# First loads, warm-up products and slab statistics at the head of a two-branch kernel

## The chip, the cores and the metric

One core of one Trainium2 chip. The metric is the device time of one execution in microseconds (us). The span that a profile shows is about 1.75 us shorter than the time of the same execution (201.1 and 202.87 us for the kernel before).

## The reference, cut to what matters

```python
def reference(A_x, A_w_r, A_w_i, B_x, B_w_gate, B_w_up, B_w_down):   # x: 1 x 2048 x 640
    x  = A_x
    xn = _layernorm(x, axis=-1)
    s  = irfft2(rfft2(xn) * (w_r + 1j * w_i))                          # spectral branch
    g  = _silu((_gelu(xn @ w_gate) * (xn @ w_up)) @ w_down)            # 640 -> 1536 -> 640
    return x + s * g
```

The kernel cuts the 2048 rows into 16 slabs of 128. The spectral branch is done by matrix products: a "fold" of each slab pair, then products with tables (T, FM, FT and others). A *gate* or *up* product is one with w_gate or w_up, a *down* product one with w_down.

## The kernel before: the parts that the argument touches

Names in the profiles: uT is the product of the gate and up branches that the down products read, ge the gelu of the gate, mb the input of a fold, BU the folds' results read back from HBM. A bank (tags sp, pg, pu) is a piece of the memory that TensorE writes to. The tail is all that follows the last product. A transfer is issued by an engine's queue and has landed when all its data are there.

A small scheduler in the kernel takes every operation with modelled durations, its inputs and buffers, and writes out one fixed order for each engine. `rank` orders what is ready at the same time.

The head. Slab 0 is loaded by ScalarE's queue, everything else by SyncE's (`dma` calls `nc.sync.dma_start`). `keep_warm` emits dummy products. `land` is the scheduler's guess of a landing time in ns.

```python
    nc.scalar.dma_start(out=X[:, 0, :], in_=xv[:, 0, :])
    ...
    load_w(Wg, gv, g_in, 0, 2, land=4690)
    load_x(1, 2, land=5200)
    load_w(Wu, uv, u_in, 0, 2, land=6790)
    load_x(2, 3, land=7280)
    load_x(3, 4, land=7750)
    t = add(blank, "DVE", (330, 400), (0, -9), new=[idle])
    t = warmed = keep_warm(6, [t])
```

The first four slabs go to TensorE untouched by the normalisation (tile XR). Their gate and up products are corrected later, when each row's mean and scale have come back from HBM, broadcast to all partitions, as the tile RB (512 KB):

```python
    rb_in = dma(RB..., D5....partition_broadcast(P), (0, -5, 1), 524288, after=[rs])
```

Of the kernel before, what the change touches and what calls it, by code (L numbers as in the profile page):

```python
# [12 lines left out]
BF16 = mybir.dt.bfloat16  # L13
ACT = mybir.ActivationFunctionType
ALU = mybir.AluOpType
P = 128
# [98 lines left out]
class Plan:  # L115
# [12 lines left out]
    def add(self, emit, eng, cost, rank, after=(), new=(), use=(), size=0, slow=1.0, hold=0, order=(), lag=0, land=0):  # L128
        engs = eng if isinstance(eng, dict) else {eng: cost}
        t = Task(emit=emit, engs=engs, rank=rank, after=list(after), new=list(new), size=size, slow=slow, hold=hold, order=list(order), lag=lag, land=land,  # L130
                 seq=len(self.tasks))
        for s in (*new, *use):
            s.users.append(t)
        self.tasks.append(t)
        return t
# [72 lines left out]
def c_pe(*ns):  # L208
    occ = sum(n / 2.4 + 2.5 for n in ns)
    return occ, occ + 240  # L210


def c_act(n, psum=True, extra=0):
    return 0.833 * n + 60 + extra, 0.833 * n + 200 + extra


def c_dve(n, rate=2, psum=False, extra=0):
    d = ((120 if psum else 58) + n / rate) / 0.96 + extra
    return d + 10, d + 130
# [3 lines left out]
def kernel(  # L223
# [11 lines left out]
    nc = tc.nc  # L235
# [32 lines left out]
    Wg = persist.tile([P, 5, F], BF16)  # L268
    Wu = persist.tile([P, 5, F], BF16)
# [7 lines left out]
    def flat(t):  # L277
        names = "abcde"[:len(t.shape) - 1]
        if len(names) == 1:
# [4 lines left out]
                uT=16, ge=3, th=2, G2=12, W=3, xb=1)  # L284
    plan = Plan(BUFS, dict(PE=700, DVE=900, ACT=3500, POOL=900, SP=750))
    add = plan.add

    def place(slot, shape, dt=BF16):
        if slot.tag in ("sp", "pg", "pu"):
            slot.tile = psum.tile([P, *shape], dt, tag=slot.tag, name=slot.tag)  # L290
        else:
            slot.tile = work.tile([P, *shape], dt, tag=slot.tag, name=slot.tag, bufs=BUFS[slot.tag])
        return slot.tile

    def copy_on(e, out, in_):
        return nc.scalar.copy(out=out, in_=in_) if e == "ACT" else nc.vector.tensor_copy(out=out, in_=in_)  # L296
# [5 lines left out]
    def dma(out, in_, rank, size, after=(), new=(), use=(), slow=1.0, land=0):  # L302
        return add(lambda e: nc.sync.dma_start(out=out() if callable(out) else out, in_=in_() if callable(in_) else in_),  # L303
                   "SP", (430, 430), rank, after=after, new=new, use=use, size=size, slow=slow, land=land)

    gv = B_w_gate.rearrange("(c p) f -> p c f", p=P)
    uv = B_w_up.rearrange("(c p) f -> p c f", p=P)
# [4 lines left out]
    x_in, g_in, u_in, tab_in, d_in = {}, {}, {}, {}, {}  # L312
# [3 lines left out]
    def load_x(a, b, land=0):  # L316
        seq[0] += 1
        t = dma(X[:, a:b, :], xv[:, a:b, :], (0, -4, seq[0]), (b - a) * 163840, use=[sX], land=land)
        for n in range(a, b):
            x_in[n] = t  # L320
# [9 lines left out]
    def load_w(sb, view, got, a, b, land=0):  # L330
        cs = slice(a * P, b * P)
        seq[0] += 1
        w = dma(sb[:, :, cs], view[:, :, cs], (0, -4, seq[0]), (b - a) * 163840, slow=1.1, land=land)
        for t in range(a, b):
            got[t] = w

    def load_gu(a, b):
        load_w(Wg, gv, g_in, a, b)
        load_w(Wu, uv, u_in, a, b)
# [15 lines left out]
    nc.scalar.activation(out=warm, in_=warm, func=ACT.Gelu_apprx_tanh)  # L355
    for w in WF:
        nc.gpsimd.memset(w[:, :, :, L:LP], 0.0)
    idle, heat = Slot("uT"), Slot("sp")

    def blank(e):  # L360
        nc.vector.memset(place(idle, (512,)), 0.0)

    def keep_warm(n, after, rank=(0, -9), ns=425):
        def go(e):
            if heat.tile is None:
                place(heat, (2, 512))
            for k in range(n):
                nc.tensor.matmul(heat.tile[:, k % 2, :], lhsT=idle.tile[:, 0:P], rhs=idle.tile,
                                 start=True, stop=True, skip_group_check=True)
        return add(go, "PE", (n * ns, n * ns), rank, after=after, new=[] if heat.users else [heat], use=[idle] + ([heat] if heat.users else []))  # L370
    seq[0] += 1
    x_in[0] = add(lambda e: None, "SP", (1, 1), (0, -5), size=1, land=3620)
    load_w(Wg, gv, g_in, 0, 2, land=4690)
    load_x(1, 2, land=5200)
    load_w(Wu, uv, u_in, 0, 2, land=6790)
    load_x(2, 3, land=7280)
    load_x(3, 4, land=7750)
    t = add(blank, "DVE", (330, 400), (0, -9), new=[idle])
    t = warmed = keep_warm(6, [t])
    load_gu(2, 4)  # L380
    load_x(4, 6)
    load_tab("f1")
# [71 lines left out]
    def turn_raw(n1):  # L454
        pt = Slot("sp")

        def half():
            return pt.tile[:, 0, :].bitcast(BF16)[:, 0:D]

        def mm(e):  # L460
            place(pt, (2, 512))
            for c in range(5):
                nc.tensor.transpose(out=half()[:, c * P:c * P + P], in_=X[:, n1, c * P:c * P + P], identity=ident)
        a = add(mm, "PE", c_pe(*[140] * 5), (0, n1), after=[x_in[n1], warmed], new=[pt], use=[sX])
        if n1 == 0:
            keep_warm(2, [a], (0, 0, 0))
        raw[n1] = add(lambda e: copy_on(e, XR[:, :, n1 * P + (n1 > 0):(n1 + 1) * P + (n1 > 0)], half().rearrange("p (c n) -> p c n", c=5)),
                      {"ACT": c_act(640)} if n1 < 2 else {"ACT": c_act(640), "DVE": (415, 560)}, None, (0, n1), after=[a], use=[pt], hold={1: 1000}.get(n1, 200))
    for n1 in range(4):
        turn_raw(n1)  # L470

# [68 lines left out]
            outs.append(add(cp, either(640), None, (1, 2 * j + s), after=[a] + outs, new=[] if s else [A], use=[pa, A] if s else [pa]))  # L540
        stored[j] = dma(lambda: D2[:, 2 * j:2 * j + 2, :], lambda: A.tile, (0, -1, j), 327680, after=outs, use=[A], slow=1.1)

    lead = ("DVE", "ACT", "DVE", "ACT")
    for n1 in range(NSLAB):
        if n1 % 2 == 0:
            xn_of[n1 // 2] = Slot("s1")
# [18 lines left out]
    t = add(rows_pe, "PE", (215, 460), (0, 7), after=[*minused, turned[2]] + [roots[n1] for n1 in range(4)], new=[sr])  # L565
    t = add(lambda e: nc.vector.tensor_copy(out=place(rt, (P,), FP32)[0:8, :], in_=sr.tile[0:8, 0, 0:P]), "DVE", c_dve(128, 1, True), (0, 3.5), after=[t], new=[rt], use=[sr])
# [303 lines left out]
    uT, u_done, xr_in, step = {}, {}, {}, [0]  # L870
# [182 lines left out]
```

## Time and profile before

| | before |
|---|---|
| time, median of 3 | 202.65 us (202.62 to 202.78) |
| span of the profiled run | 201.1 us |
| TensorE busy | 195.2 us, 97% |
| its waits ahead of the tail | 1.2 (start), 0.4 (slab 1), 0.4 us (at 37 us) |

How to read it: TensorE is the bound, so a change can win only where TensorE stands still or runs slowly. The lines themselves stand in the prediction. One view that the prediction did not look at became the important one: the order in which SyncE issues transfers. Here is that part of its timeline in the kernel before, from 43 to 56 us (start, us, queue, line, kind, output<-input, count; the first number is when the issue starts, not when the data land):

```profile
43.45 0.53 SPq L303 DMA_DIRECT2D D<-mc  x1
...
44.77 0.48 SPq L303 DMA_DIRECT2D D<-mc  x1
...
47.38 0.57 SPq L303 DMA_DIRECT2D T<-tab_t  x1
...
50.68 0.53 SPq L303 DMA_DIRECT2D D<-mc  x1
51.27 0.44 SPq L303 DMA_DIRECT2D FM<-tab_fm  x1
51.75 0.73 SPq L303 DMA_DIRECT2D FT<-tab_ft  x1
```

`D<-mc` is a fold store, 320 KB each. Every table stands *behind* the store that is ready at that moment.

### The profile page before, as it was taken

What the parts mean: (1) busy time and instruction counts of PE and PEld (TensorE: products, weight loads), DVE (VectorE), ACT (ScalarE), POOL (GpSimd) and SP (SyncE); (2) the same over time, 40 slices, a digit from 0 to 9 for tenths busy, and PEclk for the clock granted to TensorE, in tenths of its full rate; (3) what the DMA queues carried; (4) which work ended last, traced back from release to release, by engine and by line L of the source; (5) the groups of instructions that cost most, each with busy time, mean ns of one, the idle gap of its engine ahead of it and who ended that gap; (6) DMA issues with size and microseconds to landing.
All of it is one profiled execution on the core that took longest, in us unless ns stands there. A gap on an engine that the chain in (4) does not pass through costs nothing.

```text
span 201.1 us, 4125 instructions
## 1 busy us (share of the span) xinstructions
PE 195.2 (97%) x1527; PEld 117.4 (58%) x1527; DVE 149.7 (74%) x320; ACT 127.2 (63%) x224; POOL 33.1 (16%) x73
## 2 busy tenths in 40 slices
PE   7999999999999999999999999999999999999992
PEld 2994444566544555677755555467765555457781
DVE  3789969999323249999998999933257788887774
ACT  3898997974632768778775766333466565766421
POOL 2412347596000000000000000000004122211210
PEclk9999999999999999999999999999999999999999
DMA  6999999569949677333244210117704332332432
GB/s 175 329 316 325 344 392 235 126 165 196 301 128 375 223 202 178 103 93 115 61 126 126 75 50 16 68 49 221 317 3 135 96 132 100 98 107 92 130 103 65
DMA packets 35894, 32.62 MB, mean 162 GB/s; under 512 B 10910, under 2 KB 32930, under 8 KB 35874
## 3 DMA queue, kind: packets, MB, share of 16 engines
q1 hardware_dynamic: 34434, 29.49, 49.1%
q0 software_dynamic: 1152, 2.66, 4.8%
q10 hardware_dynamic: 288, 0.20, 0.5%
q8 instruction: 12, 0.20, 0.4%
q14 instruction: 8, 0.07, 0.1%
HBM read 22.51 MB, written 9.19 MB: 158 GB/s over the span
## 4 chain that ended last, share of the span: by engine, by line
PE 79%; DMA 10%; SPq 4%; DVE 3%; issue 1%; ACT 1%; DVEq 0%
PE pg L886 19%; PE pu L886 19%; PE pg L970 13%; PE pu L970 12%; DMA X<-in_A_x_dram 6%; SPq L303 4%; DMA RB<-D 4%; PE sp L697 3%; PE sp L830 3%; PE sp L772 2%; PE sp L806 2%; PE sp L670 2%; PE sp L532 1%; PE sp L690 1%; PE sp L824 1%
## 5 line engine op out<-in xcount | busy, mean ns | idle before, releaser
L886 PE MATMUL pu<-xnT,Wu 128*128 128x512 bf16 (+1 forms) x245 | 57.6, 366 | 0.0
L886 PE MATMUL pg<-xnT,Wg 128*128 128x512 bf16 (+1 forms) x245 | 57.5, 366 | 0.0
L907 DVE TENSOR_TENSOR uT<-pu,ge 128x512 bf16<-128x512 f32 x46 | 31.7, 689 | 20.9 <-PE pu L886 18.4
L970 PEld LDWEIGHTS <-uT 128*128 128x128 bf16 x396 | 37.8, 98 | 14.1 <-issue 0.6
L903 ACT ACTIVATE ge<-pg 128x512 bf16<-128x512 f32 x46 | 27.4, 597 | 25.5 <-PE pg L886 25.0
L886 PEld LDWEIGHTS <-Wg 128*128 128x128 bf16 x285 | 25.2, 98 | 22.1
L886 PEld LDWEIGHTS <-Wu 128*128 128x128 bf16 x285 | 25.1, 98 | 21.8
L970 PE MATMUL pg<-Wd,uT 128*128 128x320 bf16 (+2 forms) x204 | 30.5, 293 | 0.4 <-ACT ge L903 0.4
L970 PE MATMUL pu<-Wd,uT 128*128 128x320 bf16 (+1 forms) x192 | 29.7, 297 | 0.0
L296 ACT CAST ma<-sp 128x644 bf16<-128x644 f32 (+1 forms) x32 | 23.4, 792 | 9.7 <-PE sp L830 7.9
L932 POOL COPY xr<-s 1x1 bf16<-1x1 bf16 x1 | 0.2, 182 | 101.8 <-DVE s L856 101.8
L933 POOL DMA_DIRECT2D xr<-in_A_x_dram x16 | 8.8, 552 | 32.3 <-DVE res L957 31.7
L296 ACT CAST IU<-sp 128x640 bf16<-128x640 f32 x16 | 10.9, 691 | 4.2 <-PE sp L772 4.1
L979 ACT ACTIVATE th<-pg 128x320 f32<-128x320 f32 (+2 forms) x17 | 7.3, 427 | 9.9 <-PE pg L970 8.9
L296 ACT CAST Vt<-sp 128x640 bf16<-128x640 f32 x16 | 10.8, 691 | 3.7 <-PE sp L806 3.7
L984 DVE SCALAR_TENSOR_TENSOR G<-th,pg 128x320 bf16<-128x320 f32 (+1 forms) x16 | 7.7, 479 | 7.1 <-ACT th L979 6.9
L979 ACT ACTIVATE th<-pu 128x320 f32<-128x320 f32 (+1 forms) x16 | 7.0, 438 | 9.2 <-PE pu L970 9.0
L984 DVE SCALAR_TENSOR_TENSOR G<-th,pu 128x320 bf16<-128x320 f32 (+1 forms) x16 | 7.7, 480 | 5.6 <-ACT th L979 5.3
L296 ACT CAST mc<-sp 128x640 bf16<-128x640 f32 x15 | 9.8, 694 | 2.3 <-PE sp L533 1.3
L433 POOL TENSOR_TENSOR RSTD<-MVA,mh 128x1 f32<-128x1 f32 x12 | 8.4, 697 | 4.5 <-DVE MVA L415 3.7
L848 DVE TENSOR_TENSOR mb<-ma 128x640 bf16<-128x640 bf16 x8 | 3.9, 493 | 6.9 <-ACT ma L296 6.9
L750 DVE TENSOR_TENSOR R<-Y 64x644 bf16<-64x644 bf16 x16 | 7.8, 490 | 0.4
(107 smaller groups left out, 252.9 us busy)
## 6 DMA issues: line engine op xcount, KB each, us to landing
BU<-D SPq DMA_DIRECT2D x8, 640.0 KB
D<-mc SPq DMA_DIRECT2D x8, 320.0 KB
D<-IU SPq DMA_DIRECT2D x8, 320.0 KB
xr<-in_A_x_dram POOLq DMA_DIRECT2D x16, 160.0 KB, 2.6
out_dram<-res SPq DMA_DIRECT2D x15, 160.0 KB
Wg<-in_B_w_gate_dram SPq DMA_DIRECT2D x6, 320.0 KB
Wu<-in_B_w_up_dram SPq DMA_DIRECT2D x6, 320.0 KB
Wd<-in_B_w_down_dram SPq DMA_DIRECT2D x6, 320.0 KB
```

The lines of the kernel that those rows point to most:

```text
L296: return nc.scalar.copy(out=out, in_=in_) if e == "ACT" else nc.vector.tensor_copy(out=out, in_=in_)
L303: return add(lambda e: nc.sync.dma_start(out=out() if callable(out) else out, in_=in_() if callable(in_) else in_), "SP", (430, 430), rank ...
L433: nc.gpsimd.tensor_tensor(out=rstd, in0=var, in1=mh, op=ALU.pow)
L697: nc.tensor.matmul(into(q, ri), lhsT=sZ.tile[:, q, ri, :], rhs=FM[:, kinds[q][2] + (4 if ri and kind == 0 else 0), :], start=False, stop=T ...
L750: nc.vector.tensor_tensor(out=o, in0=Yf[:, ::-3, :], in1=Yf[:, 1:3, :], op=ALU.subtract)
L886: nc.tensor.matmul(ps.tile[:, lo:hi + more], lhsT=w[:, c, t * P:(t + 1) * P], rhs=XR[:, c, lo + (lo > 0):hi + 1 if lo or more else hi] if ...
L903: nc.scalar.activation(out=ge.tile, in_=pg.tile if src is None else src, func=ACT.Gelu_apprx_tanh)
L907: nc.vector.tensor_tensor(out=u.tile, in0=pu.tile if src is None else src, in1=ge.tile, op=ALU.mult)
L933: nc.gpsimd.dma_start(out=sx.tile, in_=xv[:, n1, :])
L970: nc.tensor.matmul(ps.tile[:, 0:hi - lo], lhsT=uT[grp, ks[i]].tile[:, j * P:(j + 1) * P], rhs=Wd[:, ks[i], lo:hi], start=(i == 0), stop=(i ...
L979: nc.scalar.activation(out=th.tile[:, 0:hi - lo], in_=ps.tile[:, 0:hi - lo], func=ACT.Tanh, scale=0.5)
L984: nc.vector.scalar_tensor_tensor(out=G2.tile[:, lo:hi], in0=th.tile[:, 0:hi - lo], scalar=1.0, in1=ps.tile[:, 0:hi - lo], op0=ALU.add, op1 ...
```

## The change

Its intent: have slabs 1 and 2 on the chip earlier, so that TensorE has real products sooner; start the dummies on a constant tile, without waiting for VectorE's memset; and take one slab's statistics off ScalarE. Cut to its core:

```diff
-    load_w(Wg, gv, g_in, 0, 2, land=4690)
-    load_x(1, 2, land=5200)
-    load_w(Wu, uv, u_in, 0, 2, land=6790)
-    load_x(2, 3, land=7280)
-    load_x(3, 4, land=7750)
-    t = add(blank, "DVE", (330, 400), (0, -9), new=[idle])
-    t = warmed = keep_warm(6, [t])
+    load_x(1, 2, land=4150)
+    load_w(Wg, gv, g_in, 0, 2, land=5210)
+    load_x(2, 3, land=5700)
+    load_w(Wu, uv, u_in, 0, 2, land=6760)
+    load_x(3, 4, land=7250)
+    t = warmed = keep_warm(7, [], ns=425)
 ...
-                nc.tensor.matmul(..., lhsT=idle.tile[:, 0:P], rhs=idle.tile, ...)
+                nc.tensor.matmul(..., lhsT=ones[:, 0:P], rhs=ones, ...)
 ...
-        if n1 == 0:
-            keep_warm(2, [a], (0, 0, 0))
 ...
-    lead = ("DVE", "ACT", "DVE", "ACT")
+    lead = ('DVE', 'DVE', 'ACT', 'DVE')
```

(`ones` is the constant 1.0 tile. Not shown: slab 1's copy may now go to VectorE too, and the scheduler's `hold` for slab 0's copy is longer.) The engines' orders change, because the scheduler runs anew.

More of the change, by code (lines that the diff above doesn't have):

```diff
@@ L357 @@
         nc.gpsimd.memset(w[:, :, :, L:LP], 0.0)
-    idle, heat = Slot("uT"), Slot("sp")
-    def blank(e):
-        nc.vector.memset(place(idle, (512,)), 0.0)
+    heat = Slot("sp")
+    ones = nc.const_aps.tensor(1.0, [P, 512], BF16)
     def keep_warm(n, after, rank=(0, -9), ns=425):
@@ L367, in go @@
             for k in range(n):
-                nc.tensor.matmul(heat.tile[:, k % 2, :], lhsT=idle.tile[:, 0:P], rhs=idle.tile,
+                nc.tensor.matmul(heat.tile[:, k % 2, :], lhsT=ones[:, 0:P], rhs=ones,
                                  start=True, stop=True, skip_group_check=True)
-        return add(go, "PE", (n * ns, n * ns), rank, after=after, new=[] if heat.users else [heat], use=[idle] + ([heat] if heat.users else []))
+        return add(go, "PE", (n * ns, n * ns), rank, after=after, new=[] if heat.users else [heat], use=[heat] if heat.users else [])
     seq[0] += 1
     x_in[0] = add(lambda e: None, "SP", (1, 1), (0, -5), size=1, land=3620)
-    load_w(Wg, gv, g_in, 0, 2, land=4690)
-    load_x(1, 2, land=5200)
-    load_w(Wu, uv, u_in, 0, 2, land=6790)
-    load_x(2, 3, land=7280)
-    load_x(3, 4, land=7750)
-    t = add(blank, "DVE", (330, 400), (0, -9), new=[idle])
-    t = warmed = keep_warm(6, [t])
+    load_x(1, 2, land=4150)
[4 more added lines that the diff above has]
+    t = warmed = keep_warm(7, [], ns=425)
     load_gu(2, 4)
@@ L464, in turn_raw @@
         a = add(mm, "PE", c_pe(*[140] * 5), (0, n1), after=[x_in[n1], warmed], new=[pt], use=[sX])
-        if n1 == 0:
-            keep_warm(2, [a], (0, 0, 0))
         raw[n1] = add(lambda e: copy_on(e, XR[:, :, n1 * P + (n1 > 0):(n1 + 1) * P + (n1 > 0)], half().rearrange("p (c n) -> p c n", c=5)),
-                      {"ACT": c_act(640)} if n1 < 2 else {"ACT": c_act(640), "DVE": (415, 560)}, None, (0, n1), after=[a], use=[pt], hold={1: 1000}.get(n1, 200))
+                      {"ACT": c_act(640)} if n1 < 1 else {"ACT": c_act(640), "DVE": (415, 560)}, None, (0, n1), after=[a], use=[pt], hold={0: 1000, 1: 1000}.get(n1, 200))
     for n1 in range(4):
```

## The prediction

> **What bounds the kernel now.** I read the page first, then the chain of waits in order of time, then who waited for whom on TensorE, then the timeline of the first 14 us and of 29 to 44 us, and the DMA view in half-microsecond stretches.
>
> The page's first part says which engine matters:
>
> ```profile
> span 201.1 us, 4125 instructions
> PE 195.2 (97%) x1527; PEld 117.4 (58%) x1527; DVE 149.7 (74%) x320; ACT 127.2 (63%) x224; POOL 33.1 (16%) x73
> ```
>
> TensorE is busy 195.2 of 201.1 us. Busy alone would not prove a bound, so I checked the spacing: in the chain a group of five 128x512 products takes 1.08 us, 216 ns each, although one product is recorded as 366 ns on average. Groups follow each other at that spacing from about 50 us to 197 us. TensorE there is really full, and no other engine can shorten that stretch. The only time to win is where TensorE does no useful work. The list of what TensorE waited for has three entries:
>
> ```profile
> PE sp L368 <- DVE uT L361: 1.2, 1, 1.2
> PE sp L463 <- DMA X<-in_A_x_dram: 0.4, 1, 0.4
> PE pg L970 <- ACT ge L903: 0.4, 1, 0.4
> ```
>
> The rest of the 5.9 us of idle is the tail behind the last product (about 4 us from 197.2), which has the same code and order in both kernels. The head, before the kernel's first useful stream, reads so:
>
> ```profile
> 1.21 2.74 PE L368 MATMUL sp<-uT 128*128 128x512 bf16 x6 [1.21 <-DVE uT L361]
> 3.75 0.72 PE L463 MATMUL sp<-ident,X 128*128 128x128 bf16 x5
> 4.28 0.62 PE L368 MATMUL sp<-uT 128*128 128x512 bf16 x2
> 4.50 0.69 ACT L296 COPY XR<-sp 128x640 bf16<-128x640 bf16 x1 [1.83 <-PE sp L463]
> 5.30 0.45 PE L463 MATMUL sp<-ident,X 128*128 128x128 bf16 x5 [0.41 <-DMA X<-in_A_x_dram]
> 5.59 0.73 PE L886 MATMUL pg<-XR,Wg 128*128 128x129 bf16 x10
> ```
>
> Six dummy products, the transposes of slab 0, two more dummies, a wait for slab 1, its transposes, and only at 5.59 us the first gate products. From there TensorE is packed: the timeline has 13 to 40 products in every 2 us and no idle note until 37.49 us. That last one is
>
> ```profile
> 37.49 0.97 PE L970 MATMUL pg<-Wd,uT 128*128 128x320 bf16 x6 [0.38 <-ACT ge L903]
> ```
>
> and the chain leads it back through ScalarE and VectorE to one transfer, the broadcast RB:
>
> ```profile
> 22.20 7.48 DMA RB<-D
> ...
> 32.92 1.30 DVE IU L920
> ```
>
> **What the Trainium skill says.** (1) "TensorE: Matmul & The Clock Gate", Part 1 (the clock gate): a cold array takes 426.7 ns for 512 columns, and turns fast after some 3.4 us of activity, at a moment that depends on a free-running window. The trace agrees: six dummies take 2.74 us; the two dummies at 4.28 end at 4.90 us, which is one warm spacing plus one latency, so the array was already fast there. (2) The same page, Part 4 (PE-mode transpose), says that transposes do not count as busy in the same way. No view here settles that; it is a risk below. (3) "Perfetto Trace Analysis", Identifying the Most-Contended Engine: matmul busy share is a poor measure because products are pipelined; the 216 against 366 ns here agree. (4) "DMA: Bandwidth & Descriptors", Issuing engines are not separate DMA queues: loads issued by ScalarE and SyncE share the same 16 engines. The DMA view agrees: between 3.0 and 3.5 us both queues move packets, and the engines are full (109 to 118% mean busy share from 3 us on).
>
> **The change, part by part.**
>
> *Load order.* Before, the queue brings slab 0, gate weights, slab 1, up weights, slabs 2 and 3; after, slabs 0 and 1, gate weights, slab 2, up weights, slab 3. Slabs are 160 KB and weight pieces 320 KB. Prefix sums in KB, before: slab 1 complete at 640, up weights at 960, slab 2 at 1120. After: slab 1 at 320, gate weights at 640, slab 2 at 800, up weights at 1120, slab 3 at 1280 as before. In the trace 640 KB landed when slab 1 woke TensorE, at 5.30 us. So the gate weights will land at about 5.25 to 5.3 us, slab 1 about 1 us earlier than before (near 4.2 us or less), slab 2 near 5.8, and the up weights half a microsecond later than now (160 KB at the view's 313 to 322 GB/s), near 6.8 us.
>
> *Dummies.* VectorE's memset at 0.88 us goes; the constant tile is written at 0.30 us, ahead of the start, so the dummies can begin at about 0.78 us. Seven cold ones need 7 x 0.427 = 2.99 us and end at 3.77; now six start at 1.21 and end at 1.21 + 2.56 = 3.77. Slab 0 lands at 3.74 in both. Nothing won, nothing lost; activity simply starts 0.43 us earlier. The two dummies at 4.28 go, and slab 1's transposes take their place, 4.28 to about 4.8.
>
> *First gate products.* They need slab 0's copy (4.50 + 0.69 = 5.19 us, unchanged) and the gate weights (5.25 to 5.3). So they start at about 5.32 instead of 5.59: **0.27 us won**, which is slab 1's transposes (0.28) moved into time that was dummies and waiting. Then 10 gates (0.56 us, at 56 ns), slab 2's transposes (0.28) and 10 gates (0.56) bring TensorE to about 6.75, where the up weights must be there. Now it starts them at 6.82 with one group of five fewer done. Even with the up weights at 6.85 the lead is 0.28 - 0.03 = 0.25 us.
>
> *Statistics D D A D.* One slab's statistics move from ScalarE (0.74 + 0.19 + 0.83 + 0.19, nearly 1.8 us with gaps) to VectorE (0.89 + 0.21 + 0.15 = 1.25 us); in exchange the scheduler gives ScalarE three to four of the early copies (0.49 to 0.69 us each). The last of the four normalised slabs is ready near 10.6 us instead of 11.84. I walked the orders of both engines up to 14 us with these durations: TensorE has to wait at no place by more than 0.1 us. Sum at 14 us: 0.2 to 0.25 us ahead.
>
> *The stall at 37 us.* RB has the same bytes ahead of it on the saturated queue (all slabs, all gate and up weights, three pieces of Wd, one store), so it lands at about 29.7 us again. What changes is VectorE's order behind it. Now the second IU product ends at 34.81 + 0.68 = 35.49. In the new order two fewer long pieces stand ahead of it: seven instructions from 29.71 at spacings of 0.60 to 0.67 give 34.2, or 34.85 if one is stretched to 1.3 as the IU one is now. From its end ScalarE needs 1.92 us (35.52 to 37.44) until the gate bank is free: 36.15 to 36.8. TensorE, 0.25 us ahead but with one more fold pair (0.55 us) already done, comes there at 37.11 - 0.25 + 0.55 = 37.4. So the 0.38 us stall should vanish: **0.38 us more**.
>
> *Later.* Every product remains; the two dummies fewer and one more cost nothing outside the head. The folds end one pair earlier and the spectral products stand two gate groups (2.2 us) earlier in TensorE's order. Their input, BU, is issued now at 57.7 us and first used at 65.8, so the slack is about 6 us after the transfer's own time; I expect no wait. Expected sum: 0.25 + 0.38 = 0.63 us. I take 0.1 off for small new waits that the static reordering may bring: about 0.55 us, 202.65 - 0.55 = 202.1 us.
>
> **Rivals.** *A: DMA-bound head.* The chain shows that the stretch up to 30 us hangs on the transfers (RB from 22.20), whose total does not change. Then the lead of 0.25 us is swallowed by the 37 us stall and the time is 202.6. For it: full DMA queues until 30 us. Against: VectorE's shorter way behind RB. *B: the clock stays slow.* Without dummies beside them, the transposes at 3.75 to 4.8 may not keep the array warm, and the gates at 5.3 run at 107 instead of 56 ns for up to a microsecond: 0.3 to 0.5 us back, 202.5. Against: 3 us of dummies already warmed it before, and they start earlier now. *C: reordering helps or hurts downstream.* VectorE is full from 16 to 52 us, so a group that the scheduler put earlier can now meet its input late; two waits of half a microsecond would give 203. *D: up weights late*, by the slowest DMA engine: another 0.2 to 0.4 us at 6.8, 202.4.
>
> **Range and chances.** A, B and D each cost at most the gain; C is the only way above 203. I give the full gain (201.9 to 202.2) about half, A, B or D (202.2 to 202.6) a third, C the rest: 80% in 201.6 to 202.9. Two per cent is 4 us, and all idle of TensorE ahead of its tail sums to 2 us, so faster by over 2% can hardly be; slower by as much would need a stall that nothing here points to.
>
> **What would show it.** In the new profile: dummies from about 0.78 us; slab 1's transposes right behind slab 0's; first gate product near 5.3; the first up product near 6.8 with no idle note over 0.2 us; RB landing near 29.7; no idle note at 37 us; the last product ending about 0.6 us earlier. The prediction is wrong if TensorE shows a new wait of 0.5 us or more in 30 to 70 us, or early gates spaced at 107 ns.

## More of the kernel before

Medians are over 3 to 11 executions.

The folds. Each copies two product tiles (tag "sp", 2 buffers) into one output tile A (tag "mc", 2 buffers), and SyncE stores A to HBM. A's buffer is free again only when that store has landed:

```python
    BUFS = dict(sp=2, pg=2, pu=2, s1=4, ma=2, mb=2, mc=2, Y=1, ...)
    ...
            outs.append(add(cp, either(640), None, (1, 2 * j + s), after=[a] + outs, new=[] if s else [A], ...))
        stored[j] = dma(lambda: D2[:, 2 * j:2 * j + 2, :], lambda: A.tile, (0, -1, j), 327680, after=outs, use=[A], slow=1.1)
```

Three tables of the spectral branch, T, FM and FT (512, 241.5 and 80.5 KB), go through the same queue at a low rank, once the fourth store is done:

```python
    for k in ("t2", "fm", "ft"):
        load_tab(k, (0, 1, seq[0]), after=[stored[3]])
```

## The result, and the profile after

| | before | after |
|---|---|---|
| time, median of 4 | 202.72 us (202.62 to 202.83) | 204.47 us (204.29 to 204.56) |
| span of the profiled run | 201.1 us | 202.5 us |
| start of the last group of products | 196.34 us | 197.75 us |

The ratio is 1.0085 (95% interval 1.0068 to 1.0103). A ratio is the mean time of one kernel's fast runs over that of the other's of the same rounds, so not quite the ratio of the medians quoted. The two profiled executions took 202.87 and 204.29 us, 1.42 us apart; the medians are 1.75 us apart. What follows accounts for the profiles; the other 0.3 us is not accounted for. The changed kernel is within 2%, but slower, and outside the predicted range.

The changed kernel's page, first part, shows what busy time hides. TensorE is busy as long as before (195.3 against 195.2 us) in a longer span:

```profile
span 202.5 us, 4102 instructions
...
PE 195.3 (96%) x1509; PEld 118.0 (58%) x1526; DVE 147.7 (73%) x319; ACT 126.9 (63%) x224; POOL 35.3 (17%) x73
```

What TensorE waited for in the changed kernel (waiting tile, releaser: us in total, times, longest):

```profile
PE sp L528 <- ACT mc L296: 1.2, 1, 1.2
PE sp L367 <- PEq L1033: 0.8, 1, 0.8
PE pg L882 <- ACT XR L296: 0.2, 1, 0.2
```

The waits for slab 1 and at 37 us are gone, as meant. The first line is new, and larger than both together.

TensorE's timeline of the changed kernel, first 8 us:

```profile
0.77 3.15 PE L367 MATMUL sp<-const-bfloat16-1.0 128*128 128x512 bf16 x7 [0.77 <-PEq L1033]
4.02 1.25 PE L461 MATMUL sp<-ident,X 128*128 128x128 bf16 x10
5.51 1.22 PE L882 MATMUL pg<-XR,Wg 128*128 128x129 bf16 x10 [0.25 <-ACT XR L296]
6.55 0.47 PE L461 MATMUL sp<-ident,X 128*128 128x128 bf16 x5
6.86 0.73 PE L882 MATMUL pg<-XR,Wg 128*128 128x128 bf16 x10
7.42 0.73 PE L882 MATMUL pu<-XR,Wu 128*128 128x129 bf16 x10
```

Slab 0's transposes start at 4.02 us instead of 3.75, and the first ten gates take 1.22 us instead of 0.73: the array runs cold until about 6.5 us. Cold means here: ten products take 1.04 us from start to start (5.51 to 6.55), where the next ten take 0.56 (6.86 to 7.42). The page's granted clock reads 1.00 in both stretches, so only the spacing shows it. At the first 512-column gate TensorE is at 14.54 us against 14.23: 0.31 us behind.

The new wait, in three views of the changed kernel. TensorE's timeline:

```profile
48.01 1.79 PE L966 MATMUL pg<-Wd,uT 128*128 128x320 bf16 x12
51.03 0.38 PE L528 MATMUL sp<-mb,F1T 128*128 128x512 bf16 x1 [1.22 <-ACT mc L296]
```

ScalarE's timeline (a fold's copies from the product bank to the output tile):

```profile
50.28 1.29 ACT L296 CAST mc<-sp 128x640 bf16<-128x640 f32 x2 [1.64 <-DMA D<-mc]
```

And SyncE's issues:

```profile
42.63 0.57 SPq L303 DMA_DIRECT2D T<-tab_t  x1
43.26 0.42 SPq L303 DMA_DIRECT2D FM<-tab_fm  x1
43.78 0.38 SPq L303 DMA_DIRECT2D D<-mc  x1
44.20 0.44 SPq L303 DMA_DIRECT2D FT<-tab_ft  x1
```

Read upwards: the tables T and FM, 753.5 KB, now stand *ahead* of a fold store, where before they stood behind one. The chain of waits of the changed kernel gives that store's time to landing and what hung on it:

```profile
43.78 6.48 DMA D<-mc
50.28 0.70 ACT mc L296
51.03 0.38 PE sp L528
```

The store lands at 50.26 us. Until then ScalarE has no output buffer for a later fold, so it does not empty the product bank, so TensorE has no bank for the next fold. The Trainium skill, "DMA: Bandwidth & Descriptors", Queues, rings and completion order, says that on each DMA engine descriptors are consumed in ring order; a store queued behind 753.5 KB landing 6.48 us after its issue agrees with that. The order is not the whole of the 6.48 us, though. In the trace a landing is 16 events, one for each piece of a transfer. Of that store 15 pieces were in by 48.48 us, 4.70 us after the issue; the last came at 50.26. (In a_tabs, below, where no table stands just ahead of it, all 16 pieces of the fifth store were in after 2.66 us.) ScalarE was free for the copy from 48.65 us, so without the last piece TensorE would hardly have waited: an estimate from these times. a_spare shows the same straggler (48.45 and 50.67 us). What held it back is open.

**Balance.** To see every loss, noted or not, I took the spacing of TensorE's starts from 28 to 54 us and subtracted what the products take when packed (0.81 us for six 320-column products, for example). That also finds waits which the idle note makes too small or omits, because a product's modelled end covers them. Before: 0.54 + 0.14 us around 37 us. After: none there (0.08 us at 39 us is left out), but 0.19 + 0.16 us ahead of two folds at 40.5 and 43.7 us, and 1.38 us at 51.03 us. Sum of the changes: head 0.31 + 1.38 + 0.35 - 0.68 = 1.36 us, of the 1.41 us by which the last products start later. From 54 us on the two kernels take the same time for the same work.

### The profile page after: what moved, and what is told of

It reads as the page before. It is cut to its first block, busy times and chain, and to the rows that moved or that the text cites. A ratio compares the mean times of both kernels' runs of the same rounds, so it can differ in the third digit from the quotient of the medians.

```text
span 202.5 us, 4102 instructions
## 1 busy us (share of the span) xinstructions
PE 195.3 (96%) x1509; PEld 118.0 (58%) x1526; DVE 147.7 (73%) x319; ACT 126.9 (63%) x224; POOL 35.3 (17%) x73
## 3 DMA queue, kind: packets, MB, share of 16 engines
q0 software_dynamic: 1152, 2.66, 5.1%
## 4 chain that ended last, share of the span: by engine, by line
PE 92%; DMA 5%; ACT 1%; issue 1%; DVE 0%; DVEq 0%
PE pg L882 26%; PE pu L882 25%; PE pu L966 12%; PE pg L966 11%; DMA D<-mc 3%; PE sp L693 3%; PE sp L826 3%; PE sp L768 2%; PE sp L802 2%; PE sp L666 2%; DMA X<-in_A_x_dram 2%; PE sp L528 1%; PE sp L686 1%; PE sp L820 1%; PE sp L461 1%
## 5 line engine op out<-in xcount | busy, mean ns | idle before, releaser
L882 PE MATMUL pu<-xnT,Wu 128*128 128x512 bf16 (+1 forms) x237 | 56.7, 365 | 0.4
L882 PE MATMUL pg<-xnT,Wg 128*128 128x512 bf16 (+1 forms) x236 | 56.6, 365 | 0.4
L882 PEld LDWEIGHTS <-Wg 128*128 128x128 bf16 x285 | 25.9, 99 | 24.5 <-issue 0.4
L966 PE MATMUL pu<-Wd,uT 128*128 128x320 bf16 (+1 forms) x192 | 29.7, 297 | 0.0
L296 ACT CAST mc<-sp 128x640 bf16<-128x640 f32 x16 | 10.7, 695 | 2.6 <-DMA D<-mc 2.5
L953 DVE TENSOR_TENSOR res<-yg,xr 128x640 bf16<-128x640 bf16 (+1 forms) x17 | 7.9, 462 | 1.7 <-DMA xr<-in_A_x_dram 1.6
L296 ACT CAST Z<-sp 128x1024 bf16<-128x1024 f32 x8 | 7.9, 1017 | 0.8 <-PE sp L666 0.8
```

Of the source, the lines that this page charges most:

```text
L296: return nc.scalar.copy(out=out, in_=in_) if e == "ACT" else nc.vector.tensor_copy(out=out, in_=in_)
L882: nc.tensor.matmul(ps.tile[:, lo:hi + more], lhsT=w[:, c, t * P:(t + 1) * P], rhs=XR[:, c, lo + (lo > 0):hi + 1 if lo or more else hi] if ...
L953: (nc.gpsimd if n1 in () else nc.vector).tensor_tensor(out=res.tile[:, lo:hi], in0=yg.tile[:, lo:hi], in1=sx.tile[:, lo:hi], op=ALU.add)
L966: nc.tensor.matmul(ps.tile[:, 0:hi - lo], lhsT=uT[grp, ks[i]].tile[:, j * P:(j + 1) * P], rhs=Wd[:, ks[i], lo:hi], start=(i == 0), stop=(i ...
```

## The experiments

Twelve kernels ran, in three sets, each with runs of the kernel before on the same chip (medians 202.80, 202.96 and 203.06 us). Unless said otherwise, only the named instruction moves and all other orders stay as they were. The balance of each profiled run, in us, next to its timing:

| run | head: first 512-column gate | waits, 28 to 54 us | last products | median time | ratio to before (95%) |
|---|---|---|---|---|---|
| before | 14.23 | 0.68 | 196.34 | 202.72 | 1 |
| after | 14.54 | 1.73 | 197.75 | 204.47 | 1.0085 (1.0068 to 1.0103) |
| a_tabs | 13.93 | 0.97 | 196.33 | 203.02 | 1.0012 (0.9996 to 1.0029) |
| a_spare | 14.27 | 0.69 | 196.43 | 202.90 | 1.0000 (0.9988 to 1.0012) |
| b_tabs | 14.11 | 1.44 | 196.95 | 204.18 | 1.0071 (1.0037 to 1.0104) |
| a_both | 16.40 | 0 | 197.76 | 203.91 | 1.0046 (1.0031 to 1.0062) |
| a_rb | 14.08 | 2.26 | 197.76 | 204.83 | 1.0087 (1.0071 to 1.0103) |
| b_rb | 14.18 | 0 | 195.53 | 202.66 | 0.9983 (0.9970 to 0.9996) |
| a_rb2 | 14.61 | 0.62 | 196.75 | 203.6 | 1.0013 (0.9995 to 1.0031) |
| a_sp0 | 14.69 | 0.36 | 196.54 | 204.1 | 1.0048 (1.0022 to 1.0074) |
| a_all | 14.78 | 1.07 | 197.28 | 204.19 | 1.0053 (1.0040 to 1.0067) |
| b_ones | 14.15 | 0.76 | 196.34 | 202.86 | 0.9990 (0.9972 to 1.0008) |

In each row, the differences to "before" in columns one and two add up to that of column three within 0.1 us: 14.69 - 14.23 + 0.36 - 0.68 = 0.14 for a_sp0, 0.20 measured. So head and these waits are the whole difference in where the last products of these profiled runs start. (Two runs with another instruction order, p_load and p_lead, are told below.)

The tail differs too. From the start of the last products to the end of the span, before, after, a_tabs, a_spare, b_ones and p_lead take 4.7 to 4.8 us, b_tabs and a_both 4.9, and a_rb, b_rb, a_rb2, a_sp0, a_all and p_load 5.2. It is the last store to HBM: it is issued at 198.59 us in the kernel before and at 197.77 in b_rb, and the span ends 2.50 and 2.97 us later. So b_rb's profile gains 0.81 us on TensorE and gives 0.47 of it back. Whether this belongs to a kernel or is a draw is open.

The profiled run is one draw, and not always a middling one: the runs of a_sp0 took 203.51, 204.60, 203.66 and 204.55 us, and the profile is of the first.

### Is the table order the cause? Move the tables back (a_tabs)

```diff
+        put(tab_in["t2"], stored[4])      # T right behind the fifth fold store
+        put(tab_in["ft"], stored[5])      # FM and FT behind the sixth
+        put(tab_in["fm"], stored[5])
```

> The changed kernel with one thing moved: on the SyncE queue the three spectral tables (T, FM, FT) go out behind the store of the fifth and sixth fold, as in the kernel before, not ahead of it; every other engine's order is the changed kernel's. Theory 1 (the loss is the 1.2 us wait of TensorE near 50 us, made by table loads queued ahead of a fold store whose landing frees the mc buffer): that wait goes, time 204.45 - 1.2 to 1.5 = about 203.1 (203.0 to 203.4). Rival (the slow clock and late slab at the head set the time): no change, about 204.4. Second rival (many small later waits): between, 203.7 to 204.2.

The wait for mc is gone, and most of the loss with it: 203.02 us, as the theory had it. (Its profile also drew a warm head, first ten gates in 0.73 us; a_spare's, next, did so only in part.) In its waits only this is left between 10 us and the tail:

```profile
PE pg L966 <- DVE uT L903: 0.3, 2, 0.2
```

### Is it the buffer? One more output buffer, tables left where they are (a_spare)

The seventh fold's output goes into a tile that is idle then; the changed kernel's order of every engine is kept.

```diff
+                    folds.append(A)
+                    A.tag = "Y" if len(folds) == 7 else "mc"
```

> The changed kernel in its own order, tables still ahead of the store; only the seventh fold's output tile lies in a buffer that is idle then (tag Y), so its copy does not wait for the store at all. Theory 1: the wait of TensorE near 50 us goes as well, time about 203.1. If the late store itself mattered through the reload of BU at 56 us, the time would stay near 204.4 with a new wait at the first BU product (65 us).

202.90 us, ratio 1.0000. The tables still stand ahead of the store, and yet TensorE no longer waits: the copy that had to wait 1.64 us for the store's landing runs at once, into Y:

```profile
48.60 1.28 ACT L296 CAST Y<-sp 128x640 bf16<-128x640 f32 x2
```

The two repairs act on different links of one chain (the late landing, the buffer that waits for it), and each alone removes the wait. That rules out that the fold's own input was late.

### Does the order alone slow the kernel before? (b_tabs)

```diff
+        put(tab_in["t2"], stored[4], False)   # T and FM ahead of the fifth store
+        put(tab_in["fm"], stored[4], False)
```

> Positive control: the kernel before with only T and FM moved on the SyncE queue ahead of the store of the fifth fold, as the changed kernel has them. Theory 1: a copy to mc waits for that store and TensorE gets a wait of 0.3 to 1.2 us near 50 us, time 203.0 to 203.9. Rival (head): 202.7 as before.

204.18 us, ratio 1.0071: in the kernel before, two table issues moved ahead of one store cost most of what the whole change does, and more than the 203.9 expected. Its profiled run was its best but one, and shows the wait at half the size that it has in the changed kernel:

```profile
PE sp L532 <- ACT mc L296: 0.5, 2, 0.4
```

By spacing the two waits are 0.87 us, and the last products start 0.61 us late; the median time is 1.38 us over that of the kernel before. So the profile shows the sort of wait, and less than half of the loss.

### The head: both slabs on ScalarE's queue (a_both)

```diff
     nc.scalar.dma_start(out=X[:, 0, :], in_=xv[:, 0, :])
+    nc.scalar.dma_start(out=X[:, 1, :], in_=xv[:, 1, :])
```

on top of a_tabs, and slab 1's load on SyncE left out.

> As a_tabs, and slab 1 is issued by ScalarE right behind slab 0 on the same queue, so that it cannot share the engines with slab 0. Theory for the head: slab 0 lands at 3.74 us again instead of 4.01, the first gates start 0.2 to 0.3 us earlier; time 0.2 to 0.3 under a_tabs, about 202.8. Rival (the head is swallowed by a later transfer-bound wait): equal to a_tabs.

A miss. The gate weights, now first on SyncE's queue, got their packets ahead of the slabs: their first packet is at 1.8 us, slab 0's at 2.6. TensorE's timeline of this run:

```profile
4.22 0.72 PE L463 MATMUL sp<-ident,X 128*128 128x128 bf16 x5 [0.31 <-DMA X<-in_A_x_dram]
5.86 0.71 PE L463 MATMUL sp<-ident,X 128*128 128x128 bf16 x5 [0.92 <-DMA X<-in_A_x_dram]
6.37 1.29 PE L884 MATMUL pg<-XR,Wg 128*128 128x129 bf16 x10
```

The 0.92 us without products were followed by a cold array: ten gates in 1.29 us, and again in 1.27. The head ended 2.17 us late.

### The head: slab 0 ahead of slab 1 on the same queue (a_sp0)

```diff
-    nc.scalar.dma_start(out=X[:, 0, :], in_=xv[:, 0, :])
+    nc.sync.dma_start(out=X[:, 0, :], in_=xv[:, 0, :])
```

again on top of a_tabs.

> The same repaired changed kernel with slab 0 issued by the same queue as slab 1 and ahead of it, so that its packets can only go first. Theory 'slab 0 is late because slab 1's packets on the other queue overtake it': slab 0's transposes start at 3.7 to 3.8 us instead of 3.9 to 4.05, the first gates at 5.3 us as the prediction had it, whether warm or cold. Rival 'slab 0 is late because more bytes are asked for at once': still 3.9 us or later. Time: within 0.3 us of 203.0, since RB bounds the stretch to 38 us anyway.

Half a hit. Slab 0 came at 3.71 us, so it had been late because slab 1's packets on the other queue went first. But the gates did not come at 5.3:

```profile
3.71 1.02 PE L461 MATMUL sp<-ident,X 128*128 128x128 bf16 x10
5.88 0.74 PE L882 MATMUL pg<-XR,Wg 128*128 128x129 bf16 x10 [1.15 <-DMA Wg<-in_B_w_gate_dram]
```

SyncE issued the gate weights at 1.64 us, behind two slabs, instead of at 1.17 us. That is 0.47 us later, and the gates start 0.37 us later than in the changed kernel (5.88 against 5.51). The transfers also have a hole there. The table by stretches gives the rate in its last column (GB/s), between 3.0 and 3.5 us; first line the changed kernel, second this run:

```profile
3.00:3.50 0.50, 0.50 (x3) 0.01 (x1) 0.00 (x0) 0.00 (x0) 0.00 (x0) 1.00 1.10 350
```
```profile
3.00:3.50 0.50, 0.50 (x3) 0.15 (x2) 0.45 (x2) 0.00 (x0) 0.00 (x0) 1.00 0.44 106
```

So none of the orders tried has slab 0 at 3.7 us *and* the gate weights at 5.3: with two queues slab 0 comes second, with one the weights come late. Time 204.1 us, further from 203.0 than expected. In the profile the last products start 0.21 us behind those of a_tabs and the tail is 0.46 us longer; its slower executions are not explained.

### What holds TensorE near 38 us? (a_rb, b_rb, a_rb2, a_all)

In a_tabs the head led by 0.30 us at 14 us and nothing of it was left at the end. Theory: RB's landing bounds that stretch, so load it earlier. First, ahead of a fold store and a weight piece (a_rb, on top of a_tabs):

```diff
+        put(rb_in, d_in[2])
```

> As a_tabs, and the broadcast RB goes out two 320 KB transfers earlier on the SyncE queue (ahead of a fold store and a Wd piece). Theory 2 (after the table loads, what swallows any lead of the head is RB: it lands near 29.5 us in all kernels, and the last two gate groups of the first quarter can be finished only some 9.7 us after it, so TensorE waits for uT near 38.5 us when it is ahead): RB lands 1 to 2 us earlier, the waits for uT near 38.5 us (0.3 to 0.6 us in a_tabs) go, time 0.2 to 0.6 under a_tabs: 202.3 to 202.8. Rival (VectorE is full there, so its order and not RB sets it): equal to a_tabs, 203.0.

A miss, by the mechanism of the first experiments: this store, too, was pushed back behind half a megabyte. It was issued at 22.20 us instead of 20.75 and landed at 28.86 instead of 27.39.

```profile
31.08 0.38 PE L528 MATMUL sp<-mb,F1T 128*128 128x512 bf16 x1 [0.90 <-ACT mc L296]
```

The same idea in the kernel before, ahead of weight pieces only (b_rb):

```diff
+        put(rb_in, stored[0])
```

> The kernel before with RB moved two 320 KB transfers (Wd pieces) earlier. Theory 2: RB lands about 2 us earlier, the wait of 0.38 us at 37.5 us goes, time 202.8 - 0.4 = 202.4. Rival (VectorE's order sets it): 202.8.

A hit: the first correction on RB starts at 28.5 instead of 29.7 us, the stall at 37 us is gone, and behind its start TensorE waits for nothing up to the tail. Its ratio, 0.9983, makes it the only kernel of the study that beats the kernel before, by about a third of a microsecond.

Then the same edit on top of a_tabs (a_rb2), and this together with a_sp0's (a_all):

> The changed kernel with the three tables back behind the fold stores, and RB moved ahead of one piece of the down weights only, behind the first fold store (the earlier try put it ahead of a store too, which made that store late). Theory 'the head's lead is swallowed by RB': RB lands about 0.7 us earlier, the two small waits for uT near 38 us shrink from 0.3 to under 0.1 us, and the time falls from 203.0 to 202.5 to 202.8. Rival 'VectorE's own order, not RB, holds TensorE there': RB earlier, waits unchanged, time 202.9 to 203.1. If a table-like delay of a store comes back: a wait for mc near 30 us and 203.5 or more.

> All three repairs of the changed kernel: tables behind the stores, RB ahead of one weight piece, slab 0 on the queue of slab 1. If the head's lead of 0.3 us and the earlier RB both come through: 202.3 to 202.6, and no wait over 0.2 us behind 10 us. If the head runs cold: 202.6 to 202.9. If RB is not the bound: 203.0.

Both missed; neither is faster than a_tabs. But the edit did not do its work. By the last of its 16 pieces in the traces, RB landed at 29.20 us in a_rb2 and at 29.58 in a_all, against 29.45 in a_tabs, with heads 0.68 and 0.85 us behind that of a_tabs. So these two runs do not test the theory. They show VectorE's part: in a_all it began on RB only at 30.11, and the two waits for uT were as long as in a_tabs. VectorE's timeline of a_all has no idle note between 31.07 us and these waits: it is simply full. a_sp0, which has no noted wait there, shows the same. These are its VectorE and its TensorE:

```profile
40.13 0.48 DVE L515 TENSOR_TENSOR mb<-ma 128x640 bf16<-128x640 bf16 x1
```
```profile
39.65 0.98 PE L966 MATMUL pu<-Wd,uT 128*128 128x320 bf16 x6
40.66 0.39 PE L528 MATMUL sp<-mb,F1T 128*128 128x512 bf16 x1
```

Six products from 39.65 us are over at 40.46 by their spacing. The fold starts at 40.66, just behind VectorE's last piece of its input, which ends at 40.61. So in the changed kernel's order VectorE, full from RB on, sets TensorE from about 38 to 44 us. RB is not quite out of it: in a_tabs VectorE stood idle for 0.40 us until RB landed, so an earlier RB could win at most that much there (an estimate); no run shows it. (That a_rb2 had no waits for uT says nothing: TensorE came there 0.97 us later than in a_tabs.)

### One part alone (b_ones, p_lead, p_load)

The dummies on the constant tile, nothing else (b_ones):

```diff
-                nc.tensor.matmul(..., lhsT=idle.tile[:, 0:P], rhs=idle.tile, ...)
+                nc.tensor.matmul(..., lhsT=ones[:, 0:P], rhs=ones, ...)
```

> The kernel before with its eight dummy products on the constant tile and nothing else changed: they start at 0.78 instead of 1.21 us. Theory of the prediction (dummies neutral): time within 0.15 us of before, first gates at 5.6 us. If an earlier start of activity changes the clock: the first ten gates take another time than 0.73 us, and the time moves by up to 0.4 us.

Neutral, 202.86 us, with the first gates at 5.51 us, as warm as before. The statistics D D A D alone (p_lead) and the load order alone (p_load), each with the scheduler free to reorder:

> The kernel before with the statistics D D A D alone (scheduler free). The order shows T, FM and FT behind the sixth fold store, one place later than in the kernel before. Theory 1: no wait for a copy to mc near 50 us, time 202.4 to 203.0. Rival (the new statistics order is what costs): 203.5 or more.

> The kernel before with the new load order alone (old dummies, old statistics, scheduler free). The order of the SyncE queue shows T, FM and FT behind the fourth and ahead of the fifth fold store. Theory 1: a wait of TensorE for a copy to mc near 50 us, time 203.3 to 204.5. Rival (the head's new order itself is good or bad, not the tables): 202.4 to 202.8 if the head gains as predicted.

p_lead took 203.45 us (ratio 1.0025, 1.0010 to 1.0039), above its expected range, p_load 203.85 (1.0055, 1.0029 to 1.0080), inside its range. Neither profile has the wait for mc on TensorE. p_lead has two other waits near 38 us, by their notes 0.6 us for uT and 0.3 us for ge.

For p_load this is a miss in the mechanism, though the time fits: T, FM and FT were issued at 43.87, 44.48 and 44.96 us, ahead of the fifth store, as expected, and yet TensorE did not wait. The store came only 2.9 us behind FT, and the first copy that needed its buffer waited 0.21 us:

```profile
47.81 0.52 SPq L303 DMA_DIRECT2D D<-mc  x1
51.62 1.29 ACT L296 CAST mc<-sp 128x640 bf16<-128x640 f32 x2 [0.21 <-DMA D<-mc]
```

So tables ahead of a store are not enough for the wait. In the changed kernel the store follows FM by 0.5 us and is waited for from 48.65 us on; here it follows FT by 2.9 us and is waited for from 51.4. Which of the two decides was not tested.

p_load came late to its first gates (6.71 us), but its last products start at 196.40 us, 0.06 us behind the kernel before; its profiled run (203.38 us, its fastest) loses the rest in the tail. That the two excesses add up to nearly the whole is chance rather than a proof: the wait that costs most in the changed kernel is in neither.

## Why the prediction was wrong

- **The step that failed** is in "Later": "the slack is about 6 us after the transfer's own time; I expect no wait." It looked at the *inputs* of what moved on TensorE and found them early. What moved to a bad place was on SyncE: two tables ahead of a store. A wait of 1.22 us by its note, 1.38 by spacing, came from an *output* buffer that was not free. a_tabs and a_spare show it, b_tabs in part; p_load shows that the order alone does not always cost, and 1.78 us of that store's 6.48 are one late piece out of 16, which stays open. With this wait and the cold gates both of the prediction's own signs of being wrong came true. Rival C had the right sort (a reordering downstream, above 203 us), but named a late input, and I gave it too little weight.
- **The second term** is the head: "Even with the up weights at 6.85 the lead is 0.28 - 0.03 = 0.25 us." It was a lag of 0.31 us. Up products began at 7.42 us. Two things went wrong. The prefix sums took both queues as one row in the order that I wrote down, but slab 0 came at 4.02 us, behind slab 1. And rival B, which I had priced at 0.3 to 0.5 us but left out of the sum, came true: the first ten gates took 1.22 us. Rival D did not: no wait for the up weights is noted.
- **Cold or warm was a draw.** Five profiles of kernels with this head show the ten gates at 1.22 and 1.24 (cold), 0.95 (turning) and twice 0.73 us (warm); five of kernels with the old head and load order (before, b_tabs, b_rb, p_lead, b_ones) show no cold one. That is too few to say that the new head runs cold more often, and why it should is open.
- **Dummies** "nothing won, nothing lost" was right: b_ones. The statistics did what was worked out, too: the last of the four normalised slabs is ready at 10.87 us (about 10.6 was forecast, 11.84 before).
- **The stall at 37 us** vanished, as worked out, and was worth more than the 0.38 us of its note: 0.68 us by spacing. But VectorE took back 0.35 us at 40 to 44 us with late fold inputs.
- **Rival A**, a swallowed lead, was right in effect: a_tabs led by 0.30 us and ended level. Its cause was half right: I named the transfer, and in a_tabs VectorE did wait 0.40 us for RB, but from there to the late folds it is full with its own queue of work. "VectorE is full from 16 to 52 us" was misread: from 25 to 30 us it is busy 3.4 of 5 us in the kernel before. So were "13 to 40 products in every 2 us": it is 9 to 15 from 16 to 44 us. Neither bears on the result.
- With both failed terms at their measured size the sum closes: +0.31 + 1.38 + 0.35 - 0.68 = 1.36 us of 1.41.
- **Open:** the ordinary runs of p_load, b_tabs and a_sp0 are up to 1.9, 2.1 and 1.1 us longer than their profiled run. A cold or warm head, a longer wait for a store and the tail are candidates; only profiled runs could show it.

## What to carry to other kernels

When a scheduler lays out the whole program, an edit at the head can move a transfer at 43 us. Compare the issue order of the DMA queue before and after, not only TensorE's, and put every load that has time behind every store that frees a buffer. A load just ahead of a store can hold the store's buffer; it cost TensorE a wait in the changed kernel, b_tabs and a_rb, and none in p_load. If the order cannot be kept, one spare buffer did the same here. A lead at the front of a kernel is worth only what the fullest engine behind it lets through (a_tabs: 0.30 us ahead at 14 us, level at the end).

## What the Trainium skill lacked or had wrong

- "DMA: Bandwidth & Descriptors", Issuing engines are not separate DMA queues, says that issuing from several engines saves only the issuing time, usually small beside the transfer. The runs agree with the first half: with one more issue ahead of them on SyncE's queue the gate weights were issued 0.47 us later, and the gates began 0.37 us later (a_sp0). It is not small here: 0.47 us is about half of the 0.94 us that 320 KB take at the 350 GB/s measured (an estimate).
- No page that I read tells what a load queued ahead of a store does to the kernel: behind 753.5 KB of tables a 320 KB store took 6.48 us to land, its buffer stayed taken, and TensorE stood 1.22 us two engines away.
- "TensorE: Matmul & The Clock Gate", Part 1, calls the ramp under 1% of a typical kernel and says not to fit it. It agrees (1.22 against 0.73 us for ten gates, 0.5 of 202 us), but that is as large as the gain this change was after.
